# A chunked attention with a channel mix: the opening's mixes taken from TensorE to VectorE, and another order of its steps

## The chip, the cores and the metric

The kernel runs on one core of a Trainium2 chip. The metric is the device time of one execution in microseconds (us). The core's engines are TensorE (PE; its weight loads are PEld), VectorE (DVE), ScalarE (ACT), GpSimd (POOL) and SyncE (SP), which here issues nearly all DMAs. Each engine has a queue of its own and works through it in order; between engines there are semaphores.

## The reference, cut to what matters

```python
# q, k, v: (8, 8, 576, 64); attention inside chunks of 64 tokens
scores = (q_c @ k_c.T) / 8;  attn = softmax(scores)      # + 1e-9 in the denominator
x = (attn @ v_c), heads side by side                     # (8, 576, 512)
x_prev = x moved by one token, zero at the first of a batch row
xk = mu_k * x + (1 - mu_k) * x_prev
xr = mu_r * x + (1 - mu_r) * x_prev
out = sigmoid(xr @ w_r) * (relu(xk @ w_k) ** 2 @ w_v)    # w_k 512x1024, w_v 1024x512, w_r 512x512
```

The three weights come as 64-bit numbers; the kernel reads them as pairs of 32-bit words and builds fp32 values from them.

## The kernel before, in words

The 4608 tokens are worked in 18 groups of 256; a group is two tiles of 128 tokens. The large products run in three passes each, high part by high part, high by low and low by high, so each operand (weights, `xk`, `xr`, the squared values `kk`) is split: a copy rounds the high part (`f_hi`, steps `h...0` of a weight, `.1` of a mix) and a subtraction leaves the low part (`f_lo`).

The program has two stages. The **opening** loads and splits the weights and works tiles 0 to 5 up to their mixes, and groups 0 and 1 to the end. The table `START` (lines 27 to 51) sets its order by hand: each word is a step of a task with the engine that does it (`:A` ACT, `:D` DVE), and the order of the words is the order in which instructions are queued on every engine, the DMA issues on SP among them. After it come groups 2 to 17 in a fixed pattern (`GROUP`), which the diff leaves alone. The opening's tasks are:

- `nq`, `nk`, `v`: loads of q, k and v. `sw...`: load of a weight piece (1024 KB); `cw...`: two passes on ACT (lines 296 and 300) and a shift on DVE (line 303) that turn its words into fp32; `hw...`: its high part (line 141 or 143) and low part (line 314).
- `T`: transposes of q and k on PE (line 358) and the copies out of PSUM. `S`: scores (line 401), row maximum, subtraction, exponential, sum, reciprocal, scaling. `P`: transposed probabilities (465), their copy, the product with v (`xps`, 485), the column of the token before (502, 506) and the copy to `x`.
- `Mk` and `Mr`: the two mixes of a tile. `Mk.0` makes the difference `d = x - x_prev` on DVE (line 553); `Mk.1` and `Mr.0` make the mixes; then high and low parts (`.2`, `.3` of `Mk`, `.1`, `.2` of `Mr`).
- `R`: `pr`, product of `xr` with w_r (line 683) and sigmoid. `K`: `pk`, product of `xk` with w_k (line 629), relu, square, high and low part. `V`: `pv`, product with w_v (line 714).
- `W:n`: n products of a tile of zeros (`warm`, line 1220), whose result nobody reads.

For tiles 0, 1 and 2 (`ON_PE`, line 523) a mix is made on TensorE: `make_diag` writes four sets of diagonal matrices on ACT (step `dg.0`, line 536), and eight products of 128 columns add x by `mu` and `x_prev` by `1 - mu` in PSUM (`mxk` and `mxr`, line 571). For the tiles from 3 on, DVE makes `d` and then a mix by four instructions of 128 columns (line 583; two times as many where a batch row begins inside the tile).

Of the kernel before, what the change touches and what calls it, by code (L numbers as in the profile page):

```python
# [7 lines left out]
F32 = mybir.dt.float32  # L8
# [3 lines left out]
AF = mybir.ActivationFunctionType  # L12
ALU = mybir.AluOpType
# [3 lines left out]
P = 128  # L17
CH = 64
TT = 128
# [5 lines left out]


START = """
W:9 mu.0:A nq0.0 nk0.0 T0.0 T0.2 T0.1:A swr1.0 P0.3:D T0.3:A nk1.0 nq1.0 T0.4 T0.5:A swr0.0
T0.6 T0.7:A W:4 S0.0 S0.1:D S0.2:D S1.0 W:4 T1.4 S1.1:D v0.0 T1.6 S1.2:D cwr1.1:A S0.3:A S0.4:D
S0.5:D cwr1.0:A T1.5:A W:3 T1.0 S1.3:A S1.4:D S1.5:D P0.0 T1.7:A cwr1.2:D T1.2 cwr0.0:D P1.0  # L30
T1.1:A mu.1 P0.1:A T1.3:A cwr0.1:A nq2.0 P0.2 P1.1:A S2.0 T2.2 S3.0 P0.4:D P1.3:D S2.1:D v1.0
S2.2:D mu.2:A dg.0:A S3.1:D T2.0 swk0.0 S2.3:A cwr0.2:D Mk0.1 S3.2:D T2.3:A P1.2 S2.4:D
hwr1.0:A Mk1.0:D Mk0.0:D nk2.0 Mk0.2:A cwk0.0:A swk2.0 S2.5:D Mr0.0 swk1.0 cwk0.1:A P1.4:A
T2.1:A S3.3:A T2.6 Mr0.1:A hwr1.1:D Mk0.3:D P2.3:D hwr0.0:A P2.0 cwk0.2:D Mr0.2:D Mk1.1 swk3.0
Mk1.2:A Mk1.3:D T2.7:A hwr0.1:D T2.4 Mr1.0 hwk0.0:D P2.1:A Mr1.1:D hwk0.1:D R00.0 cwk2.0:A
Mr1.2:D v2.0 S3.4:D cwk1.1:A T2.5:A Mk2.0:D cwk1.0:A swv2.0 S3.5:D v3.0 cwk1.2:D cwk3.1:A P2.2
R01.0 P2.4:A cwk2.1:A K00.0 swv0.0 R00.1:A P3.3:D R01.1:A cwk3.0:A cwk2.2:D P3.0 P3.1:A K00.1:A
hwk2.0:A Mr2.0 P3.2 hwk1.0:A cwk3.2:D Mr2.1:A S4.0 P3.4:A Mk2.1 hwk2.1:D S5.0 hwk1.1:D cwv2.0:A
cwv2.1:A hwk3.0:A swv1.0 K01.0 K01.1:A K01.2:A Mk3.0:D Mr3.0:D K02.0 K00.2:A cwv2.2:D hwk3.1:D
v4.0 Mk3.1:D Mr2.2:D S4.1:D Mr3.1:A K03.0 cwv1.1:A Mr3.2:D cwv1.0:A bk3.0 Mk2.2:D Mk2.3:D  # L40
K00.3:A R10.0 S5.1:D Mk3.2:A cwv0.1:A K01.3:A hwv2.0:A K00.4:D K02.1:A K02.2:A K01.4:D K02.3:A
P4.3:D cwv0.0:A R10.1:A Mk3.3:D hwv2.1:D R11.0 K03.1:A K02.4:D K03.2:A R11.1:A K10.0 K10.1:A
swv3.0 K10.2:A cwv0.2:D K11.0 cwv1.2:D hwv0.0:A K03.3:A S4.2:D K13.0 hwv1.0:A hwv0.1:D cwv3.1:A
bq3.0 S5.2:D cwv3.0:A K10.3:A K03.4:D v5.0 hwv1.1:D V001.0 cwv3.2:D S4.3:A K13.1:A V001.1
V001.2 hwv3.0:A K10.4:D V001.3 V001.4 S4.4:D K13.2:A S4.5:D V001.5 P4.0 hwv3.1:D S5.3:A V001.6
V001.7 P4.1:A S5.4:D K13.3:A S5.5:D P4.2 K11.1:A K13.4:D D7.1:D v7.0 P5.0 P4.4:A K11.2:A
V001.8:D K12.0 V10.0 V001.9:D V11.0 K11.3:A V11.1 P5.1:A Mk4.0:D Mk4.1:D K12.1:A P5.2 K12.2:A
P5.3:D K12.3:A K11.4:D V10.1 D6.1:D K12.4:D P5.4:A Mr4.0:D V10.2 V10.3 V11.2 V11.3 Mk5.0:D
V10.4 Mk5.1:D Mr4.1:A V11.4 D7.0:D Mk4.2:A V10.5 v6.0 V10.6 V11.5 V10.7 Mk5.2:A Mk4.3:D Mr4.2:D
Mk5.3:D Mr5.0:D Mr5.1:A V11.6 D6.0:D V11.7 V11.8:D Mr5.2:D V10.8:D  # L50
"""


# [26 lines left out]
def tile_chunk_attention_channel_mix(  # L80
# [12 lines left out]
    nc = tc.nc  # L93
    B_, H, S, D = q.shape
# [3 lines left out]
    NB = DM // P  # L98
# [16 lines left out]
    mx = pool("mx")  # L115
# [4 lines left out]
    mo = pool("mo", 2)  # L120
# [3 lines left out]
    ps_o = ctx.enter_context(tc.tile_pool(name="ps_o", bufs=2, space=PSUM))  # L124

    do = Steps()
    T = {}
# [5 lines left out]
    ident = const.tile([P, P], F32, name="ident")  # L133
    make_identity(nc, ident)
    mus = mo.tile([2 * NB, P], F32, tag="relu", name="mus")
    mu2 = par.tile([P, 2, 2, NB], F32, name="mu2")
# [10 lines left out]
    def queue(e):  # L147
        return nc.scalar if e == "A" else nc.sync
# [81 lines left out]
    def load_mu():  # L230
        do.task = "mu"

        def fn(e):
            for i, mu in enumerate((mu_k, mu_r)):
                queue(e).dma_start(
                    out=mus[i * NB : (i + 1) * NB], in_=mu.rearrange("(c p) -> c p", p=P)
                )

        def f_tr(_):
            T["mu"] = ps_k.tile([P, 2 * NB], F32, tag="k", name="mu_t")  # L240
            nc.tensor.transpose(out=T["mu"], in_=mus, identity=ident[: 2 * NB, : 2 * NB])

        def f_move(e):

            x = T["mu"].rearrange("p (i c) -> p i c", i=2)
            nc.scalar.activation(mu2[:, 0], x, AF.Copy)
            nc.scalar.activation(mu2[:, 1], x, AF.Copy, scale=-1.0, bias=1.0)

        do(fn, "A")
        do(f_tr, "P")  # L250
        do(f_move, "A")
# [197 lines left out]
    def x_cuts(t):  # L449

        cut = -t * TT % S
        if 0 < cut < TT:
            return [(0, cut, 0), (cut, TT - cut, cut + 1)]
        return [(0, TT, 0)]
# [65 lines left out]

    ON_PE = (0, 1, 2)
    diag = {}

    def make_diag():
        do.task = "dg"

        def fn(e):
            for i, nm in enumerate("kr"):  # L530
                for n in range(2):
                    to = diag[nm, n] = mo.tile([P, NB, P], F32, tag="mix", name=f"diag_{nm}{n}", bufs=4)
                    for cb in range(NB):
                        col = mu2[:, n, i, cb : cb + 1]
                        if e == "A":
                            nc.scalar.activation(to[:, cb], ident, AF.Copy, scale=col)
                        else:
                            nc.vector.tensor_scalar(to[:, cb], ident, col, None, ALU.mult)

        do(fn, "D")  # L540

    def x_mix(t):
        g, tl = divmod(t, 2)
        do.task = f"Mk{t}"
        part = slice(tl * TT, (tl + 1) * TT)

        def f_d(e):
            if t in ON_PE:
                return
            d = T[f"d{t}"] = mo.tile([P, NB, TT], F32, tag="mix", name=f"d_{t}", bufs=4)  # L550
            x = xt[t]
            for s, m, c in x_cuts(t):
                engine[e].tensor_tensor(
                    d[:, :, s : s + m],
                    x[:, :, c + 1 : c + 1 + m],
                    x[:, :, c : c + m],
                    ALU.subtract,
                )

        do(f_d, "D")  # L560
        for nm, mu in (("k", muk), ("r", mur)):

            def f_mix(e, nm=nm, mu=mu):
                x = xt[t]
                if t in ON_PE:
                    m = T[f"m{nm}{t}"] = ps_o.tile([P, NB, TT], F32, tag="o", name=f"mx{nm}_{t}")
                    for cb in range(NB):
                        for s, w, c in x_cuts(t):
                            for n in range(2):
                                c0 = c + 1 - n  # L570
                                nc.tensor.matmul(  # L571
                                    m[:, cb, s : s + w],
                                    diag[nm, n][:, cb],
                                    x[:, cb, c0 : c0 + w],
                                    start=(n == 0),
                                    stop=(n == 1),
                                )
                    return
                m = T[f"m{nm}{t}"] = mo.tile([P, NB, TT], F32, tag="mix", name=f"mix{nm}_{t}", bufs=4)
                d = T[f"d{t}"]  # L580
                for cb in range(NB):
                    for s, w, c in x_cuts(t):
                        nc.vector.scalar_tensor_tensor(
                            out=m[:, cb, s : s + w],
                            in0=d[:, cb, s : s + w],
                            scalar=mu[:, cb : cb + 1],
                            in1=x[:, cb, c : c + w],
                            op0=ALU.mult,
                            op1=ALU.add,
                        )  # L590

            def f_hi(e, nm=nm):
                if f"x{nm}{g}" not in T:
                    T[f"x{nm}{g}"] = [
                        (kp if nm == "k" else rp).tile([P, NB, G], F32R, tag=f"{nm}{s}", name=f"x{nm}{s}_{g}")
                        for s in ("hi", "lo")
                    ]
                copy(e, T[f"x{nm}{g}"][0][:, :, part], T[f"m{nm}{t}"])

            def f_lo(e, nm=nm):  # L600
                hi, lo = T[f"x{nm}{g}"]
                engine[e].tensor_tensor(
                    lo[:, :, part], T[f"m{nm}{t}"], hi[:, :, part].bitcast(F32), ALU.subtract
                )

            do.task = f"M{nm}{t}"
            do(f_mix, "D")
            do(f_hi, "A")
            do(f_lo, "D")
# [563 lines left out]


    load_mu()
    make_diag()
    for t in range(6):
        if t % 2 == 0:
            load_nat(t // 2)
# [35 lines left out]
    with tc.manual_schedule():  # L1215
        for word in START.split():
            name, _, e = word.partition(":")
# [3 lines left out]
            else:  # L1221
                fn, engine_of = first.pop(name)
# [100 lines left out]
```

## Time and profile before

| | us |
|---|---|
| median of 3 runs (lowest to highest) | 572.79 (572.33 to 573.97) |
| the profiled execution, its own time | 574.04 |
| span of that execution in the trace | 572.0 |
| busy: PE, DVE, ACT, POOL | 564.0, 452.8, 356.3, 0.7 |
| first `pr` product starts at | 39.47 |
| the opening's last product ends, and group 2's pattern begins, at | 104.22 |

All times below are from the span's start. A busy time is the sum of the engine's own instructions. In the timeline a number in brackets is the idle time of the engine before the row and what ended it; a row's first number is the start, the second how long the row's instructions took from the first start to the last end, and since instructions overlap at their edges, the step from one row's start to the next is what a row costs its engine.

### The profile page before, as it was taken

To read this page: it belongs to the slowest core of one execution; us is meant where nothing else is said; L and a number is where in the kernel's file an instruction comes from. 1 tells how busy PE (TensorE), PEld (TensorE's weight loads), DVE (VectorE), ACT (ScalarE), POOL (GpSimd) and SP (SyncE) were. 2 spreads that over 40 slices of the span, in tenths; PEclk is the share of its full clock that TensorE was granted. 3 is DMA by queue.
4 is the path that set the end of the run, shared out by engine and by line. 5 is a ranking of instruction groups with operands and counts; after the bars stand their busy time and mean duration, and the time that the engine had idled before them with its cause. 6 is when DMAs were issued, how large, how long until landed. Compare 5 with 4: busy or idle time off the path is not lost.

```text
span 572.0 us, 15372 instructions
## 1 busy us (share of the span) xinstructions
PE 564.0 (99%) x6499; PEld 536.0 (94%) x6499; DVE 452.8 (79%) x753; ACT 356.3 (62%) x535; POOL 0.7 (0%) x6
## 2 busy tenths in 40 slices
PE   8899999999999999999999999999999999999997
PEld 7789999999999999999999999999999999999997
DVE  1597878899988888878787878887888788977834
ACT  4798975472938393929292929293838384747462
POOL 0000000000000000000000000000000000000000
PEclk9899999999999999999999999999999999999999
DMA  9998152343444343330234343434343411011011
GB/s 287 220 315 200 52 110 75 85 70 69 105 90 87 93 64 95 64 94 1 77 56 101 65 96 53 99 58 97 64 84 67 74 44 40 37 39 38 1 38 38
DMA packets 184276, 49.25 MB, mean 86 GB/s; under 512 B 169608, under 2 KB 176272, under 8 KB 184208
## 3 DMA queue, kind: packets, MB, share of 16 engines
q1 hardware_dynamic: 183904, 48.01, 37.3%
q8 instruction: 51, 0.84, 0.6%
q10 hardware_dynamic: 304, 0.27, 0.1%
q14 instruction: 17, 0.14, 0.1%
HBM read 38.80 MB, written 9.44 MB: 84 GB/s over the span
## 4 chain that ended last, share of the span: by engine, by line
PE 97%; DVE 2%; ACT 0%; issue 0%
PE pk L629 35%; PE pr L683 17%; PE vx L903 15%; PE vyz L903 11%; PE pv L714 6%; PE xps L1091 3%; PE s L1006 3%; PE pt L1073 2%; PE warm L1220 1%; PE trq L358 1%; PE trk L358 1%; PE s L401 1%; PE mxk L571 1%; PE mxr L571 1%; PE pt L465 0%; PE xps L485 0%
## 5 line engine op out<-in xcount | busy, mean ns | idle before, releaser
L629 PE MATMUL pk<-xkhi,wk 128*128 128x256 f32 (+1 forms) x1166 | 201.8, 276 | 0.0
L629 PEld LDWEIGHTS pk<-xkhi,wk 128*128 128x128 f32 x1166 | 176.8, 188 | 0.3
L629 PE MATMUL pk<-xklo,wk 128*128 128x256 f32 x576 | 160.0, 278 | 0.0
L629 PEld LDWEIGHTS pk<-xklo,wk 128*128 128x128 f32 x576 | 108.3, 188 | 0.1
L650 ACT ACTIVATE rr<-pk 128x512 f32<-128x512 f32 x60 | 35.3, 588 | 114.4 <-PE pk L629 114.4
L683 PE MATMUL pr<-wr,xrhi 128*128 128x512 f32 x288 | 90.4, 395 | 0.0
L903 PE MATMUL vx<-b,ks 128*128 128x256 f32 x540 | 68.5, 276 | 0.0
L903 PE MATMUL vyz<-b,kk 128*128 128x256 f32 x540 | 68.5, 276 | 0.0
L903 PEld LDWEIGHTS vyz<-b,kk 128*128 128x128 f32 x540 | 64.5, 188 | 0.0
L903 PEld LDWEIGHTS vx<-b,ks 128*128 128x128 f32 x540 | 64.5, 188 | 0.0
L683 PEld LDWEIGHTS pr<-wr,xrhi 128*128 128x128 f32 x288 | 52.7, 188 | 10.2
L683 PE MATMUL pr<-wr,xrlo 128*128 128x512 f32 x144 | 56.2, 390 | 0.0
L932 ACT ACTIVATE u<-vx 128x256 f32<-128x256 f32 x30 | 11.5, 384 | 54.3 <-PE vx L903 54.3
L741 DVE TENSOR_TENSOR kk<-rr,kk 128x1024 fp32r<-128x1024 f32 x30 | 35.4, 1222 | 10.7 <-ACT kk L887 10.6
L657 ACT ACTIVATE rr<-rr 128x512 f32<-128x512 f32 x60 | 38.0, 633 | 1.9
L741 DVE TENSOR_TENSOR xklo<-mk,xkhi 128x1024 fp32r<-128x1024 f32 x15 | 18.4, 1225 | 24.7 <-ACT xkhi L1163 24.7
L714 PE MATMUL pv<-b,kk 128*128 128x256 f32 x288 | 33.9, 277 | 0.0
L714 PEld LDWEIGHTS pv<-b,kk 128*128 128x128 f32 x288 | 33.1, 188 | 0.1
L683 PEld LDWEIGHTS pr<-wr,xrlo 128*128 128x128 f32 x144 | 27.0, 188 | 5.7
L741 DVE TENSOR_TENSOR ks<-ss,ks 128x512 fp32r<-128x512 f32 x45 | 28.3, 683 | 0.0
L1153 DVE SCALAR_TENSOR_TENSOR mk<-d,mu,x 128x256 f32<-128x256 f32 (+3 forms) x80 | 27.7, 414 | 0.4
L1153 DVE SCALAR_TENSOR_TENSOR mr<-d,mu,x 128x256 f32<-128x256 f32 (+3 forms) x80 | 27.5, 410 | 0.0
(127 smaller groups left out, 857.3 us busy)
## 6 DMA issues: line engine op xcount, KB each, us to landing
v<-in_v SPq DMA_DIRECT2D x144, 64.0 KB, 2.5
out<-sg SPq DMA_DIRECT2D x34, 256.0 KB, 2.5
q_ring<-in_q SPq DMA_DIRECT2D x192, 36.0 KB, 2.0
k_ring<-in_k SPq DMA_DIRECT2D x192, 36.0 KB, 2.1
wk_st<-in_moe_w_k SPq DMA_DIRECT2D x4, 1024.0 KB, 11.9
wv_st<-in_moe_w_v SPq DMA_DIRECT2D x4, 1024.0 KB, 7.5
wr_st<-in_moe_w_r SPq DMA_DIRECT2D x2, 1024.0 KB, 9.9
q_ring<-in_q SPq DMA_DIRECT2D x2, 512.0 KB, 6.7
```

What stands on the lines that cost most here:

```text
L358: nc.tensor.matmul(x[halves[j], hp, :], T[f"{nm}{g}"][:, j * HP + hp, r, :], ident, start=True, stop=True,)
L629: nc.tensor.matmul(pk[:, e, part], wk[a][:, cb, f * P : (f + 1) * P], xk[b][:, cb, part], start=(n == 0 and part is parts[0]), stop=(n == ...
L650: nc.scalar.activation(r, T[f"pk{g}{fp}"], AF.Relu)
L657: nc.scalar.activation(r, r, AF.Square)
L683: nc.tensor.matmul(pr, xr[a][:, cb, tl * TT : (tl + 1) * TT], wr[b][:, cb, :], start=(n == 0), stop=(n == 3 * NB - 1),)
L714: nc.tensor.matmul(T[f"pv{g}{tl}"][:, cols[c]], kk[a][:, f, tok[tl]], quarter(f // HF, c)[:, b, f % HF, :], start=(f == 0 and n == 0 and c ...
L741: nc.vector.tensor_tensor(to, x, y, ALU.subtract)
L903: nc.tensor.matmul(to, a[i][:, f, :], weight(w, j, f), start=first and f == 0 and n == 0, stop=f == HF - 1 and n == 2, skip_group_check=True,)
L932: nc.scalar.activation(T[f"u{g}"][n // 2][:, n % 2], src(), AF.Copy)
L1006: nc.tensor.matmul(T[f"s{g}"][halves[e], j, tl, hp, :], qT[halves[j], hp, cols], kT[halves[j], hp, cols], start=True, stop=True,)
L1091: nc.tensor.matmul(T[f"xps{g}"][halves[c], 2 * j + a, tl * TT + e * CH : tl * TT + (e + 1) * CH], T[f"v{2 * g + tl}"][halves[j], hp, e, :] ...
L1153: nc.vector.scalar_tensor_tensor(out=to[:, cb, s : s + w], in0=T[f"d{g}"][:, cb, s : s + w], scalar=mu[:, cb : cb + 1], in1=T[f"xg{g}"][:, ...
```

## The change

`ON_PE`, `make_diag` and the PE branch of `f_mix` go, so that tiles 0, 1 and 2 are mixed on DVE as the others are; so does the instruction that made `1 - mu`. `START` is written anew, all of it. Of 296 words of the table before, `dg.0` is gone; 23 others name another engine or now need one. The idle products are 33 instead of 20, at other places. The low parts of the weights stand on DVE before and after.

```diff
 START = """
-W:9 mu.0:A nq0.0 nk0.0 T0.0 T0.2 T0.1:A swr1.0 P0.3:D T0.3:A nk1.0 nq1.0 T0.4 T0.5:A swr0.0
...
+mu.0:A nk0.0 nq0.0 swr0.0 W:9 T0.4 T0.6 T0.5:A swr1.0 T0.7:A T0.2 T0.3:D nk1.0 T0.0 mu.1 T0.1:A
...
             nc.scalar.activation(mu2[:, 0], x, AF.Copy)
-            nc.scalar.activation(mu2[:, 1], x, AF.Copy, scale=-1.0, bias=1.0)
...
-    ON_PE = (0, 1, 2)
...
-    def make_diag():
...
         def f_d(e):
-            if t in ON_PE:
-                return
...
             def f_mix(e, nm=nm, mu=mu):
                 x = xt[t]
-                if t in ON_PE:
...
-                                nc.tensor.matmul(
-                                    m[:, cb, s : s + w],
-                                    diag[nm, n][:, cb],
-                                    x[:, cb, c0 : c0 + w],
...
-    make_diag()
```

Steps that change between ACT and DVE once DVE's row maximum of tile 0 has begun: from ACT to DVE `Mr2.1`, `K01.2`, `K03.3`, `hwv3.0` (two instructions), `K13.3`, `K11.1`, `K12.1`, `K12.2`, `Mk4.2`, `Mk5.2`, `Mr5.1`; from DVE to ACT `P0.4`, `hwk0.0`, `Mr1.1`, `Mk2.2`.

PE, from the product with v of tile 0 on, before (the first number in a name is the group, or for `trq0`, `trq1` the row of a pair and then the group; `mxk_0` is the mix of tile 0):

```order
L485 MATMUL xps_0_314<-pT_0_308,v_0_242 64x64 x16
L401 MATMUL s_1_332<-kT_123,qT_122 64x64 x16
L358 MATMUL trq1_2_349<-ident_109,q_ring_116 64x128 x8
L401 MATMUL s_1_332<-kT_123,qT_122 64x64 x16
L358 MATMUL trq0_2_408<-ident_109,q_ring_116 64x128 x8
L571 MATMUL mxk_0_421<-x_0_160,diag_k0_387 128x128
L571 MATMUL mxk_0_421<-x_0_160,diag_k1_392 128x128
```

and PE from the same product on in the change:

```order
L484 MATMUL xps_0_292<-pT_0_287,v_0_214 64x64 x16
L357 MATMUL trq0_1_320<-ident_109,q_ring_116 64x128 x8
L357 MATMUL trq1_1_329<-ident_109,q_ring_116 64x128 x8
L464 MATMUL pt_0_275<-ident_109,p_0_210 128x128 x4
L1183 MATMUL warm_108<-idle_106 128x128 x3
L400 MATMUL s_1_372<-kT_123,qT_122 64x64 x16
L1183 MATMUL warm_108<-idle_106 128x128 x5
L400 MATMUL s_1_372<-kT_123,qT_122 64x64 x16
L484 MATMUL xps_0_292<-pT_0_287,v_1_344 64x64 x16
L647 MATMUL pr_0_0_440<-wr0_120,xrhi_0_363 128x512
```

The mixes are gone from PE, the transposes of group 2's q and k stand behind the first `pr` instead of ahead of it, and the first `pr` follows the product with v of tile 1 directly.

DVE around the low part of w_r's first piece, before:

```order
L435 TENSOR_TENSOR p_1_383<-p_1_383,z_2_448 128x512
L314 TENSOR_TENSOR wr1_121<-wr1_st_158,wr0_120 128x1024
L602 TENSOR_TENSOR xklo_0_456<-mxk_0_421,xkhi_0_455 128x4x128
L506 COPY x_1_491<-x_0_160 128x4
L303 SCALAR_TENSOR_TENSOR wk0_st_417<-wk0_st_417 128x1024
L602 TENSOR_TENSOR xrlo_0_487<-mxr_0_462,xrhi_0_486 128x4x128
```

and in the change (`d_0`, `mixr_0`, `mixk_0` belong to tile 0, `z_1` and `p_0` to the probabilities of tile 1):

```order
L313 TENSOR_TENSOR wr1_121<-wr0_st_130,wr0_120 128x1024
L428 TENSOR_REDUCE z_1_311<-p_0_210 128x8
L429 TENSOR_SCALAR z_1_311<-z_1_311 128x8
L430 RECIPROCAL z_1_311<-z_1_311 128x8
L531 TENSOR_TENSOR d_0_317<-x_0_206 128x512
L434 TENSOR_TENSOR p_0_210<-p_0_210,z_1_311 128x512
L547 SCALAR_TENSOR_TENSOR mixr_0_339<-d_0_317,mu2_115,x_0_206 128x128 x4
L547 SCALAR_TENSOR_TENSOR mixk_0_355<-d_0_317,mu2_115,x_0_206 128x128 x4
```

The difference and both mixes of tile 0 now stand in DVE's queue, between the softmax of tile 1 and the low parts.

SP's first loads before (w_r, q, k and v; `x4` is the four parts of a v tile):

```order
L184 DMA q_ring_116<-in_q 128x8x128
L184 DMA k_ring_117<-in_k 128x8x128
L292 DMA wr1_st_158<-in_moe_w_r 128x2x1024
L184 DMA k_ring_117<-in_k 128x8x128
L184 DMA q_ring_116<-in_q 128x8x128
L292 DMA wr0_st_175<-in_moe_w_r 128x2x1024
L199 DMA v_0_242<-in_v 64x4x64 x4
```

and in the change:

```order
L184 DMA k_ring_117<-in_k 128x8x128
L184 DMA q_ring_116<-in_q 128x8x128
L291 DMA wr0_st_130<-in_moe_w_r 128x2x1024
L291 DMA wr1_st_160<-in_moe_w_r 128x2x1024
L184 DMA k_ring_117<-in_k 128x8x128
L199 DMA v_0_214<-in_v 64x4x64 x4
L184 DMA q_ring_116<-in_q 128x8x128
L291 DMA wk3_st_281<-in_moe_w_k 128x4x512
L199 DMA v_1_344<-in_v 64x4x64 x4
L291 DMA wk0_st_349<-in_moe_w_k 128x4x512
```

Both pieces of w_r come ahead of the second k, and two pieces of w_k ahead of the q and k of group 2.

## Rows read from the trace of the kernel before

**Rows 1.** The page: busy time and share, then the chain by engine

```profile
PE 564.0 (99%) x6499; PEld 536.0 (94%) x6499; DVE 452.8 (79%) x753; ACT 356.3 (62%) x535; POOL 0.7 (0%) x6
...
PE 97%; DVE 2%; ACT 0%; issue 0%
```

**Rows 2.** Windows: stretch, length, busy PE, PEld, DVE, ACT, POOL, clock, DMA, GB/s

```profile
11.43:39.47 28.04, 24.49 (x379) 21.44 (x380) 19.18 (x32) 23.16 (x45) 0.00 (x0) 0.94 1.03 280
39.47:70.00 30.53, 30.53 (x325) 27.86 (x323) 23.54 (x40) 27.46 (x37) 0.00 (x0) 1.00 0.57 131
70.00:104.22 34.22, 34.22 (x350) 33.70 (x348) 26.67 (x61) 21.36 (x36) 0.00 (x0) 1.00 0.39 93
104.22:140.00 35.78, 35.78 (x452) 34.21 (x452) 33.50 (x43) 17.44 (x25) 0.00 (x0) 1.00 0.45 81
```

**Rows 3.** Timeline of PE: start, us, line, op, out<-in, records, idle before

```profile
12.90 0.69 PE L401 MATMUL s<-kT,qT 64*64 64x64 f32 x32 [1.54 <-DVE p L421]
13.52 1.16 PE L1220 MATMUL warm<-idle 128*128 128x128 f32 x8
14.61 1.97 PE L358 MATMUL trk<-ident,k_ring 128*64 128x128 f32 x32
...
21.35 0.69 PE L485 MATMUL xps<-pT,v 64*64 64x64 f32 x32 [0.53 <-ACT pT L141]
23.35 1.04 PE L401 MATMUL s<-kT,qT 64*64 64x64 f32 x32 [1.31 <-ACT pT L141]
24.32 1.97 PE L358 MATMUL trq<-ident,q_ring 128*64 128x128 f32 x16
26.23 0.99 PE L401 MATMUL s<-kT,qT 64*64 64x64 f32 x32
27.15 1.09 PE L358 MATMUL trq<-ident,q_ring 128*64 128x128 f32 x16
28.18 2.05 PE L571 MATMUL mxk<-x,diag_k 128*128 128x128 f32 x16
30.16 0.69 PE L485 MATMUL xps<-pT,v 64*64 64x64 f32 x32
...
39.47 0.70 PE L683 MATMUL pr<-wr,xrhi 128*128 128x512 f32 x2
...
52.11 2.05 PE L571 MATMUL mxk<-x,diag_k 128*128 128x128 f32 x16
54.09 0.69 PE L401 MATMUL s<-kT,qT 64*64 64x64 f32 x32
```

**Rows 4.** Windows around the stretch in which the granted clock was low

```profile
23.35:27.00 3.65, 3.65 (x78) 3.20 (x80) 0.00 (x0) 3.63 (x15) 0.00 (x0) 0.53 1.10 292
27.00:30.00 3.00, 3.00 (x48) 2.76 (x40) 2.67 (x4) 2.50 (x8) 0.00 (x0) 1.00 1.07 325
```

**Rows 5.** Timeline of DVE: a row maximum, a mix, and two instructions that follow

```profile
11.43 0.69 DVE L413 TENSOR_REDUCE m<-s 128x8 f32<-128x512 f32 x1 [10.41 <-PE s L401]
...
54.56 1.14 DVE L583 SCALAR_TENSOR_TENSOR mixr<-d,mu,x 128x128 f32<-128x128 f32 x4
55.62 1.22 DVE L303 SCALAR_TENSOR_TENSOR wv_st<-wv_st 128x1024 int32<-128x1024 int32 x1
...
63.93 0.69 DVE L602 TENSOR_TENSOR xklo<-mxk,xkhi 128x512 fp32r<-128x512 f32 x1
64.54 0.68 DVE L413 TENSOR_REDUCE m<-s 128x8 f32<-128x512 f32 x1
```

**Rows 6.** Timeline of ACT: half of the diagonal matrices

```profile
25.82 2.43 ACT L536 ACTIVATE diag_r<-ident,mu 128x128 f32<-128x128 f32 x8
```

**Rows 7.** Windows of the first 30 us, read for their last number, GB/s

```profile
0.00:20.00 20.00, 17.37 (x236) 15.57 (x236) 7.50 (x15) 9.93 (x13) 0.70 (x6) 1.00 0.93 257
20.00:30.00 10.00, 8.16 (x151) 7.07 (x149) 3.53 (x6) 8.78 (x25) 0.00 (x0) 0.83 0.97 265
```

More of the change, by code (lines that the diff above doesn't have):

```diff
@@ L27 @@
 START = """
-W:9 mu.0:A nq0.0 nk0.0 T0.0 T0.2 T0.1:A swr1.0 P0.3:D T0.3:A nk1.0 nq1.0 T0.4 T0.5:A swr0.0
[L29 to L50, printed above, removed]
+mu.0:A nk0.0 nq0.0 swr0.0 W:9 T0.4 T0.6 T0.5:A swr1.0 T0.7:A T0.2 T0.3:D nk1.0 T0.0 mu.1 T0.1:A
@@ new lines @@
+cwr0.1:A W:1 S0.0 cwr0.0:A P0.3:D S0.1:D S0.2:D S0.3:A cwr0.2:D v0.0 S0.4:D W:7 S1.0 nq1.0 W:5
+T1.6 S1.1:D cwr1.1:A mu.2:A S0.5:D S1.2:D T1.4 P0.0 hwr0.0:A swk3.0 cwr1.0:A T1.7:A S1.3:A
+cwr1.2:D P0.1:A W:3 P0.2 T1.5:A hwr0.1:D S1.4:D P0.4:A hwr1.0:A Mk0.0:D S1.5:D T1.0 T1.2 T1.1:A
+Mr0.0:D v1.0 swk0.0 P1.0 Mk0.1:D T1.3:A P1.3:D P1.1:A Mr0.1:A nk2.0 cwk3.0:A W:3 S2.0 Mr0.2:D
+S2.1:D nq2.0 W:5 S3.0 P1.2 P1.4:A hwr1.1:D v2.0 S2.2:D R00.0 S2.3:A cwk0.0:A T2.4 cwk3.1:A
+S3.1:D Mk1.0:D S2.4:D Mr1.0:D cwk0.1:A S2.5:D T2.5:A T2.6 S3.2:D swk2.0 swk1.0 Mk0.2:A Mr1.1:A
@@ new lines @@
+P2.0 T2.7:A T2.2 Mk1.1:D cwk0.2:D T2.0 Mk0.3:D P2.1:A Mk1.2:A S3.3:A Mr1.2:D T2.3:A P2.2
+cwk3.2:D hwk0.0:A hwk0.1:D Mk1.3:D T2.1:A S3.4:D P2.3:D hwk3.0:A cwk2.0:A cwk2.1:A S3.5:D
+hwk3.1:D P2.4:A v3.0 R01.0 cwk2.2:D cwk1.1:A P3.3:D cwk1.0:A K00.0 K00.1:A P3.0 cwk1.2:D
+hwk2.0:A K03.0 P3.1:A S4.0 hwk1.0:A Mk2.0:D hwk2.1:D P3.2 K03.1:A swv1.0 K00.2:A P3.4:A v5.0
+Mr2.0:D K03.2:A hwk1.1:D Mr2.1:D S5.0 Mk2.1:D K02.0 R00.1:A Mk3.0:D Mr2.2:D cwv1.0:A swv0.0
+Mr3.0:D swv2.0 K00.3:A Mk3.1:D K01.0 K00.4:D R01.1:A cwv1.1:A Mk2.2:A K03.3:D Mr3.1:A Mr3.2:D
@@ new lines @@
+v4.0 K01.1:A Mk3.2:A K03.4:D K01.2:D Mk2.3:D Mk3.3:D cwv2.0:A cwv2.1:A K02.1:A R10.0 cwv2.2:D
+cwv0.0:A R11.0 K10.0 S4.1:D cwv1.2:D K02.2:A K11.0 cwv0.1:A hwv2.0:A K01.3:A cwv0.2:D K01.4:D
+hwv0.0:A P4.3:D bq3.0 K10.1:A K10.2:A hwv2.1:D K12.0 hwv1.0:A swv3.0 R10.1:A hwv0.1:D S4.2:D
+R11.1:A S5.1:D V001.0 S4.3:A hwv1.1:D S5.2:D V001.1 V001.2 V001.3 S4.4:D K02.3:A K10.3:A S4.5:D
+S5.3:A K02.4:D cwv3.0:A S5.4:D P4.0 V001.4 cwv3.1:A S5.5:D K12.1:D P4.1:A cwv3.2:D P5.0
+hwv3.0:D P5.1:A V001.5 P4.2 hwv3.1:D K12.2:D P5.2 K12.3:A P4.4:A K10.4:D bk3.0 K11.1:D Mk4.0:D
@@ L51 @@
+V001.6 K11.2:A V001.7 K11.3:A K13.0 D7.0:D V001.9:D K11.4:D P5.3:D V001.8:D K12.4:D V11.0 V11.1
+V10.0 v6.0 Mr4.0:D K13.1:A V10.1 K13.2:A V10.2 P5.4:A K13.3:D V10.3 V11.2 V10.4 Mk4.1:D Mk5.0:D
+K13.4:D V10.5 V11.3 V11.4 V11.5 Mk4.2:D V11.6 Mk5.1:D Mr4.1:A Mr4.2:D V10.6 v7.0 D7.1:D V11.7
+D6.0:D Mk4.3:D D6.1:D Mk5.2:D Mr5.0:D V11.8:D Mk5.3:D Mr5.1:D V10.7 V10.8:D Mr5.2:D
 """
@@ L519, in att_values @@
         do(f_x, "A")
-    ON_PE = (0, 1, 2)
-    diag = {}
-    def make_diag():
[L527 to L540, printed above, removed]
     def x_mix(t):
@@ L564, in f_mix @@
                 x = xt[t]
-                if t in ON_PE:
[L566 to L570, printed above, removed]
-                                nc.tensor.matmul(
-                                    m[:, cb, s : s + w],
-                                    diag[nm, n][:, cb],
-                                    x[:, cb, c0 : c0 + w],
[L575 to L578, printed above, removed]
                 m = T[f"m{nm}{t}"] = mo.tile([P, NB, TT], F32, tag="mix", name=f"mix{nm}_{t}", bufs=4)
```

## The prediction, made before the changed kernel was run

> **What bounds the kernel now.** I read the page first: PE is busy for 564.0 of 572.0 us, and 97% of the chain that ended last is PE [rows 1]. So the span is PE's work plus PE's waits, and a change counts by what it does to either. The windows by stage come next [rows 2]: from the first `pr` at 39.47 on PE is busy for the whole of every stretch (30.53 of 30.53, 34.22 of 34.22, 35.78 of 35.78), so its waits all lie ahead of 39.47, and what the change can win lies in the opening, which ends at 104.22. Last I read PE's own timeline there [rows 3]. It shows three things to be won: the mixes on PE, three waits in brackets, and a stretch in which rows of one kind take longer than the same kind elsewhere. DVE is the engine to watch. It was idle for 28.04 - 19.18 = 8.86, 6.99 and 7.55 us of the opening's three stretches, and for only 2.28 of the 35.78 us behind it [rows 2].
>
> **Mixes removed from PE.** The first `mxk` costs 1.98 us from its start at 28.18 to the next row at 30.16, the last one 1.98 (52.11 to 54.09) [rows 3]. There are six such groups (two mixes of three tiles), the other four cost between 1.81 and 1.98, and all six 11.6 us. PE has no cover for them, so their whole cost leaves PE's work: **-11.6**.
>
> **The low clock.** [...] PE had waited 0.53 and 1.31 us just before [rows 3]. In it, one group of transposes took 1.91 us (24.32 to 26.23) where the next took 1.03 (27.15 to 28.18), and two halves of scores took 0.97 and 0.92 where the half at 12.90 took 0.62 [rows 3]: 0.88 + 0.35 + 0.30 = 1.5 us. In the change the waits there are filled with eleven idle products and with the two groups of transposes that now follow tile 0's product with v, so I take the stretch as gone: **-1.5**, with 0 as the other end.
>
> **Old waits and new idle products.** The three waits of 1.54, 0.53 and 1.31 us [rows 3] make 3.4 us, and the places where they stood now hold other work: -3.4. There are 33 idle products instead of 20; four of them cost 13.52 to 14.61 = 1.09 us [rows 3], so 13 more cost 13 x 0.27 = **+3.5**. The two cancel: the idle products are waits under another name. Work that is only moved past the first `pr` (the transposes of group 2, the transposed probabilities of tile 2) costs PE the same on either side.
>
> PE's own sum is thus -11.6 - 1.5 - 3.4 + 3.5 = -13.0 us, plus whatever PE has to wait anew for the engines that feed it.
>
> **What DVE takes over.** Per tile one difference and two mixes. A 512-wide instruction of two tensors costs 64.54 - 63.93 = 0.61 us, a mix 55.62 - 54.56 = 1.06 [rows 5]; 0.61 + 2 x 1.06 = 2.73, and three tiles 8.2. Of steps that change between ACT and DVE behind 11.43, twelve 512-wide instructions come to DVE and four leave it: eight times 0.61 = 4.9. DVE's work in the opening grows by 13.1 us. Its idle time from 11.43 to 104.22 was 8.86 + 6.99 + 7.55 = 23.4 us [rows 2], and it can't begin earlier, since its first row maximum needs the first scores, whose loads and transposes stand where they stood. So if DVE never idled any more and all its opening work ended with the opening, the opening could be 23.4 - 13.1 = 10.3 us shorter and no more. PE would gain 13.0 without that limit, so new waits of **at least 2.7** are to be expected. ACT is no such limit: it loses both rows of diagonal matrices, 2.43 us for one [rows 6], and eight steps on balance, and was idle for 4.88 + 3.07 + 12.86 = 20.8 us of the opening [rows 2].
>
> **How much PE waits.** That is the one term with no row of its own. The lower bound is the 2.7 above; it could be undercut only by DVE work that slides past the opening, at most the 2.28 us that DVE idles from 104.22 to 140 [rows 2], which gives 0.4. For the upper bound I take DVE's best-filled stretch in the trace, the same one: 2.28 of 35.78 is 6.4% idle [rows 2]. An opening that ends ten microseconds earlier has DVE at work for some 82 us, 6.4% of them is 5.2, and 2.7 + 5.2 = 7.9. I take **+3.6**, near the lower bound, for a reason in the order: what DVE does last in the opening are mixes and low parts of tile 5, which PE wants only in the stretch behind, so the opening need not end with DVE. At the front, where the change puts DVE's wait on x of tile 0, the difference of tile 0 stands behind the shift and the low part of w_r, so that wait has cover; if w_r were late, the cover would be gone and that wait would cost what x is late.
>
> **Loads.** DVE and ACT now wait for weights earlier, so I check what lands when. The DMA engines moved 257 GB/s in the first 20 us and 265 in the next ten [rows 7]: 5.14 MB by 20 and 7.79 by 30. In the new order w_r, both k and q of groups 0 and 1, both v and two pieces of w_k make 6.5 x 1.05 = 6.8 MB, down by 26.3 us. The first `pk` stands behind two `pr` and the transposes, at 35 or later, and its weights take one shift and one low part on DVE (1.2 us each) and three passes on ACT. Some 3 us are left. Moving the loads past each other on SP thus costs nothing unless they are slower by more than that.
>
> **The sum.** -13.0 + 3.6 = -9.4 us. Made against the profiled execution it is 572.0 - 9.4 = 562.6 for the span, 564.6 for its own time of 574.04. That execution was 1.25 us over the median, so against the median of 572.79 I forecast **563.4**.
>
> **Rivals.**
> *DVE sets the pace.* DVE's idle share stays what its best stretch shows, PE waits 7.9, the gain is 13.0 - 7.9 = 5.1: **567.7**. For it: DVE's queue is in order, and its first steps on each weight wait for a landing and for ACT, with every mix behind them. Against it: the new order gives DVE softmax work of tiles 1 to 3 to do in between, and in the trace the 20 us in which DVE idled most (11.43 to 39.47) are just those which the mixes now fill.
> [...]
> *A late load holds DVE's queue, and the kernel gets slower.* The shift of the first w_k piece stands on DVE ahead of the low parts of both tiles of group 0, so if that piece lands late, both `pr` and all `pk` wait behind it. It decides from the point where PE's new waits pass 13.0 us, that is when the piece lands some 3 + 13 = 16 us after 26.3; at 18 us late it costs 15 and the result is **574.8**. Against it: 7.79 MB were down by 30 us [rows 7], and the order of the loads alone doesn't take bandwidth away.
> *The change doesn't shorten the opening.* If PE's gap were only refilled, because scores, softmax and landings set the first `pr` near 36, the gain would be the 3 us between: **569.8**. Against it: ahead of the first `pr` at 39.47 PE was busy for 24.49 of 28.04 us [rows 2], largely with work that is now gone or behind it.
>
> **How the numbers follow.** The forecast has a chance of 0.70, DVE's pace 0.16, the clock 0.08, the late load 0.03, the refilled gap 0.03. The range reaches to DVE's pace above (567.7) and to the lower bound of the waits below (13.0 - 0.4 = 12.6 gained, 560.2, of which I leave out the last part): 560.9 to 568.0. It holds the forecast's own spread, the clock's case and DVE's pace at its price; what lies beyond these prices, with the last two rivals, I put at 2 in 10. A measurement of this kernel can tell about 0.3%, 1.7 us, from no change. Faster by more than that: the first three, 0.94, and the part of the refilled gap's case that lies over 1.7 us, 0.95 in all; slower 0.03, and 0.02 within.
>
> **What would show it.** Right: the first `pr` starts at 25 to 28 (39.47 less four mixes, 7.7, four groups of transposes now behind it, 4 x 1.03, and the low clock's 1.5, is 26.2), no L571 rows, the opening's last product ends near 95, DVE is idle for under 3 us between 11 and 95, PE's waits behind the first `pr` sum to 1 to 4 us and end with DVE or ACT. Groups 2 to 17 take as long as before. Wrong: a first `pr` past 31, waits of PE on DVE that go on into the stretch behind the opening, or a granted clock under 1 in more than one stretch of the opening.

## The result, and the profile after

The changed kernel takes **562.68 us** (median of 6 runs, 562.42 to 562.91); the kernel before, run beside it, 572.85 (572.33 to 574.07). The ratio is **0.9818**, 95% interval 0.9805 to 0.9831: 1.8% faster. The forecast was 563.4 with a range from 560.9 to 568.0. The profiled execution after took 562.54 us with a span of 560.8, and lies at its kernel's median; the one before lay 1.25 over its own. So the spans differ by 11.2 us, the medians by 10.2.

The page after: busy time by engine, and the chain by engine, to be held against [rows 1].

```profile
PE 554.0 (99%) x6429; PEld 526.6 (94%) x6429; DVE 462.8 (83%) x789; ACT 346.0 (62%) x509; POOL 0.7 (0%) x6
...
PE 90%; ACT 7%; DMA 2%; DVE 0%; issue 0%; ACTq 0%
```

Windows of both kernels, the opening from DVE's first row maximum on and the rest (stretch, length, busy PE, PEld, DVE, ACT, POOL, clock, DMA, GB/s). Before:

```profile
11.43:104.22 92.79, 89.24 (x1048) 83.00 (x1048) 69.39 (x131) 71.97 (x116) 0.00 (x0) 0.98 0.64 162
104.22:572.00 467.78, 464.53 (x5331) 443.52 (x5330) 383.18 (x620) 279.50 (x413) 0.00 (x0) 1.00 0.32 67
```

and after:

```profile
10.85:92.93 82.08, 79.89 (x983) 74.35 (x983) 78.42 (x165) 62.53 (x92) 0.00 (x0) 1.00 0.76 184
92.93:560.80 467.87, 464.55 (x5331) 443.53 (x5330) 383.51 (x622) 279.44 (x413) 0.00 (x0) 1.00 0.32 66
```

The rest takes 467.8 us in both, so all of the gain lies in the opening, which ends 11.3 us earlier. These rows split it: 0.6 because the first row maximum begins earlier (only half of it is shown to come from the change, as told further down), 9.35 of PE's busy time (89.24 to 79.89), and 1.4 of PE's idle time (3.55 to 2.19). DVE took on 9.0 us of work in a stretch 10.7 us shorter: its idle time fell from 23.4 to 3.7 us.

PE's timeline after, around the first `pr` and at the opening's end (start, us, line, op, out<-in, records, idle before):

```profile
22.15 0.69 PE L400 MATMUL s<-kT,qT 64*64 64x64 f32 x32
22.77 1.38 PE L1183 MATMUL warm<-idle 128*128 128x128 f32 x10
24.18 0.69 PE L400 MATMUL s<-kT,qT 64*64 64x64 f32 x32
24.69 0.65 PE L484 MATMUL xps<-pT,v 64*64 64x64 f32 x32
25.27 0.73 PE L647 MATMUL pr<-wr,xrhi 128*128 128x512 f32 x2
...
92.93 1.16 PE L970 MATMUL s<-kT,qT 64*64 64x64 f32 x64
```

No mix stands there any more; the halves of scores take 0.69 us each, where two of them took 1.04 and 0.99 in [rows 3]; the first `pr` begins at 25.27 instead of 39.47. What PE still waits for, all of its waits up to 140 us (us in total, times, longest; the first one is the start of the program):

```profile
PE warm L1183 <- DVE idle L130: 1.1, 1, 1.1
PE trk L357 <- DMA k_ring<-in_k: 1.0, 1, 1.0
PE pt L464 <- DVE p L434: 0.5, 1, 0.5
PE s L400 <- ACT pT L141: 0.3, 1, 0.3
PE pk L593 <- ACT relu L614: 0.2, 1, 0.2
PE s L400 <- ACT qT L141: 0.2, 1, 0.2
```

### The profile page after: what moved, and what is told of

It is laid out like the page before. It is cut to its first block, busy times and chain, and to the rows that moved or that the text cites. A ratio compares the mean times of both kernels' runs of the same rounds, so it can differ in the third digit from the quotient of the medians.

```text
span 560.8 us, 15239 instructions
## 1 busy us (share of the span) xinstructions
PE 554.0 (99%) x6429; PEld 526.6 (94%) x6429; DVE 462.8 (83%) x789; ACT 346.0 (62%) x509; POOL 0.7 (0%) x6
## 4 chain that ended last, share of the span: by engine, by line
PE 90%; ACT 7%; DMA 2%; DVE 0%; issue 0%; ACTq 0%
PE pk L593 32%; PE pr L647 16%; PE vx L867 15%; PE vyz L867 11%; PE pv L678 6%; PE xps L1055 3%; PE s L970 3%; PE pt L1037 2%; DMA k_ring<-in_k 2%; PE warm L1183 1%; ACT wk L141 1%; ACT wv_st L295 1%; PE trk L357 1%; ACT wv_st L299 1%; ACT relu L614 0%; ACT wk_st L299 0%
## 5 line engine op out<-in xcount | busy, mean ns | idle before, releaser
L647 PEld LDWEIGHTS pr<-wr,xrhi 128*128 128x128 f32 x288 | 52.7, 188 | 10.3
L705 DVE TENSOR_TENSOR kk<-rr,kk 128x1024 fp32r<-128x1024 f32 x30 | 35.4, 1222 | 10.7 <-ACT kk L851 10.6
```

What stands on the lines that cost most here:

```text
L647: nc.tensor.matmul(pr, xr[a][:, cb, tl * TT : (tl + 1) * TT], wr[b][:, cb, :], start=(n == 0), stop=(n == 3 * NB - 1),)
L705: nc.vector.tensor_tensor(to, x, y, ALU.subtract)
```

## The experiments

The theory: the gain is PE's work (mixes and slow stretch gone), the order's part is to give DVE the mixes early enough that PE doesn't wait for them; what limits now is DVE. Rivals: the order alone makes the gain, by better overlap; or the idle products matter; or a load does. Ratios are against the kernel before, run on the same chip.

**The mixes alone.** The order of before, with the mixes on DVE:

```diff
-S2.2:D mu.2:A dg.0:A S3.1:D
+S2.2:D mu.2:A S3.1:D
...
-Mk0.1 S3.2:D
+Mk0.0:D Mk0.1 S3.2:D
```

and likewise `Mk1.0` moved ahead of `Mk1.1`, `Mk2.0` ahead of `Mr2.0`, and `Mr2.2` ahead of `Mk3.1`.

> The mixes of tiles 0 to 2 go to VectorE as in the change, but the order of the opening stays that of before (four words moved, so that a difference comes ahead of its mixes and a buffer is free in time). Theory (TensorE's work falls by 11.6 us, but only an order that gives VectorE the mixes early turns that into time): VectorE gets 8.2 us more in a queue laid out without them, ahead of the w_k parts; TensorE, which never waits behind the first pr in the kernel before, waits there for 6 to 10 us in all; 569 to 577 us, so no gain worth the name. Rival (taking work off the engine that bounds is enough): 561 to 564 us, waits behind the first pr under 3 us.

Measured: 578.7 us, ratio 1.0093 (1.0074 to 1.0112), above the theory's range. The same mixes taken off PE make the kernel 0.9% *slower*. The two largest waits of PE:

```profile
PE pr L647 <- DVE wr L313: 4.7, 1, 4.7
PE pt L464 <- DVE p L434: 3.7, 1, 3.7
```

DVE's timeline ahead of the longest one, which ended at 43.64:

```profile
39.21 0.68 DVE L531 TENSOR_TENSOR d<-x 128x512 f32<-128x512 f32 x1
39.92 1.14 DVE L547 SCALAR_TENSOR_TENSOR mixk<-d,mu,x 128x128 f32<-128x128 f32 x4
41.76 0.69 DVE L566 TENSOR_TENSOR xklo<-mixk,xkhi 128x512 fp32r<-128x512 f32 x1 [0.70 <-ACT xkhi L141]
42.37 1.22 DVE L313 TENSOR_TENSOR wr<-wr_st,wr 128x1024 fp32r<-128x1024 f32 x1
```

The low part of w_r stands in DVE's queue behind the difference and a mix of tile 1, and behind a wait for ACT. Meanwhile the granted clock fell:

```profile
33.90:47.60 13.70, 7.81 (x30) 5.71 (x31) 12.93 (x27) 10.47 (x15) 0.00 (x0) 0.50 1.07 315
```

At a granted clock of 1.00 PE would have saved up to about half of the 7.81 us that it worked there, 3.9 (an estimate: one group of transposes in [rows 3] took 1.91 us where the granted clock was 0.53 and the next 1.03 where it was 1.00, [rows 4]). On the pages PE's idle time grew from 572.0 - 564.0 = 8.0 to 576.8 - 556.8 = 20.0 us, and its busy time fell by 7.2 us and not by the 11.6 of the mixes. The difference of 4.4 is put down to the low clock, near its estimate: -11.6 + 4.4 + 12.0 = +4.8, by which the span grew. Behind the first `pr` PE waited for 7.2 us, within the theory's 6 to 10; the low clock was not in the theory. So taking work from PE gains nothing by itself; it needs the rewritten order. Which part of that order counts (the places in the queues, the steps that go to another engine, or the loads) no run separates.

**PE's time given back.** After, with eleven idle products behind each of four places where the old kernel had a mix on PE:

```diff
-Mr0.0:D v1.0
+Mr0.0:D W:11 v1.0
```

and the same behind `Mk0.1:D`, `Mr1.0:D` and `Mk1.1:D`.

> The changed kernel with TensorE's load given back: four times eleven idle products (44 x 0.27 = 11.9 us) where the mixes of tiles 0 and 1 are queued, two of the four ahead of the first pr and two behind it. Theory (TensorE's work is what the time is made of): they fill the 2 us or so of waits that the changed kernel has and cost the rest, 6 to 10 us: 569 to 573 us. Rival (the gain comes from the new order, which starts the weights and the first pr earlier, and not from the mixes): under 565 us.

Measured: 570.35 us, ratio 0.9946 (0.9929 to 0.9964), so 7.3 us of the gain are gone. One of the four places in PE's timeline (an idle product makes two records, so 22 records are eleven products):

```profile
33.58 2.72 PE L1183 MATMUL warm<-idle 128*128 128x128 f32 x22
36.23 1.09 PE L357 MATMUL trk<-ident,k_ring 128*64 128x128 f32 x16
```

Eleven products cost 36.23 - 33.58 = 2.65 us. On the pages PE is busy for 564.1 us instead of 554.0, so all 44 cost some 10.1; the waits behind the first scores vanish in exchange (none is left but 0.2), and the span grows by 568.7 - 560.8 = 7.9. So the order alone is not the gain: with PE's time put back, most of it goes.

**No idle products.** After, with `W:9` alone left of the `W` words.

> The changed kernel without its idle products, but for the nine at the start. Theory (they stand in waits for softmax and copies): each becomes a wait of the same length, the first pr starts where it did (25.3 us), and the time is 562 to 563.5 us. [...]

Measured: 563.14 us, ratio 0.9820 (0.9803 to 0.9838), the same as after. The granted clock did fall, twice:

```profile
14.30:17.70 3.40, 3.40 (x29) 2.79 (x24) 3.40 (x5) 2.34 (x4) 0.00 (x0) 0.50 1.10 339
24.50:27.90 3.40, 3.26 (x67) 2.95 (x68) 3.08 (x5) 1.21 (x3) 0.00 (x0) 0.50 1.09 197
```

and waits stood where the idle products had been, the three largest being

```profile
PE s L400 <- DVE p L420: 1.5, 1, 1.5
PE trk L357 <- DMA k_ring<-in_k: 1.5, 2, 1.1
PE s L400 <- DVE m L412: 1.3, 1, 1.3
```

The time is the theory's, though the granted clock, which is 1.00 all through the opening of after, falls to 0.50 without the idle products. The first `pr` began at 26.55 and the opening ended at 93.83, 0.9 later than after; against that the span grew by 0.8 and the ratio by 0.0002. The pages tell why so little is left. The 24 products that are gone cost 6.75 us in after, but PE's busy time fell by only 554.0 - 550.4 = 3.6, so the other 3.1 are put down to the low clock (an estimate: at 0.50, half of the 6.66 us that PE worked in the two stretches, 3.3). PE's idle time grew by 4.4 us, from 6.8 to 11.2. The waits are thus shorter than the products in whose place they stand, against the theory, and the low clock takes back what that saves.

**The load that PE waits for, earlier.** `nk2.0` (k of group 2) moved ahead of `swk0.0` (a piece of w_k):

```diff
...
-swk0.0 P1.0 Mk0.1:D T1.3:A P1.3:D P1.1:A Mr0.1:A nk2.0
+nk2.0 swk0.0 P1.0 Mk0.1:D T1.3:A P1.3:D P1.1:A Mr0.1:A
...
```

> The changed kernel with the k of group 2 loaded ahead of the w_k piece that precedes it, so that the one wait of TensorE for a load (1.0 us, at 29.3) goes. Theory (the DMA engines run full until 52 us, so a load that is moved up moves another back): the wait turns up again at the first products with w_k, and the time is 562.5 to 564.5 us. Rival (the place of that one load costs 1.0 us): 561.5 to 562 us.

Measured: 565.17 us, ratio 0.9860 (0.9839 to 0.9882), 2.4 us *slower* than after. PE's wait for k is gone, and two others stand in its place. First PE's timeline, then ACT's, which tells why:

```profile
33.29 1.09 PE L357 MATMUL trq<-ident,q_ring 128*64 128x128 f32 x16 [1.67 <-ACT kT L141]
34.83 1.09 PE L357 MATMUL trq<-ident,q_ring 128*64 128x128 f32 x16 [0.44 <-ACT kT L141]
```

```profile
29.51 1.19 ACT L295 ACTIVATE wk_st<-wk_st 128x1024 f32<-128x1024 f32 x1 [2.44 <-DMA wk_st<-in_moe_w_k]
30.60 2.13 ACT L299 ACTIVATE wk_st<-wk_st 128x1024 int32<-128x1024 uint32 x2
32.63 0.60 ACT L141 ACTIVATE kT<-trk 128x512 f32<-128x512 f32 x1
```

ACT waits for the weight piece, which is now later, and the copy `kT` that PE needs stands behind its three passes. The rival (the wait for k was worth its 1 us) fell. The theory had the direction; the size was too small (564.5 at most) and the place another, since the wait stands ahead of q's transposes and not at the products with w_k. On the pages PE's idle time grew by 1.2 us and its busy time by 1.2. The idle time is what the edit explains; 0.7 of the busy time lie ahead of the first row maximum, before the load that was moved, and what the rest is no run shows.

**More and less work on DVE.** First the differences of tiles 0 to 2 made three times, 3.7 us of DVE work more:

```diff
-                engine[e].tensor_tensor(
+                for _ in range(3 if t < 3 else 1):
+                    engine[e].tensor_tensor(
...
```

> The changed kernel with the difference of tiles 0, 1 and 2 made three times instead of once: six more VectorE instructions of 0.61 us, 3.7 us of work for nothing. Theory (VectorE is filled to the brim in the opening, so what it gets more TensorE waits for): 2 to 4 us longer, 564.7 to 567 us. Rival (the 3.7 us for which VectorE is still idle between 11.4 and 94 take it up): 562.5 to 563.3 us.

Measured: 566.93 us, ratio 0.9886 (0.9865 to 0.9908), 3.9 us over after. PE's two long waits, and behind the first one two halves of scores:

```profile
22.11 0.66 PE L464 MATMUL pt<-ident,p 128*128 128x128 f32 x4 [1.94 <-DVE p L434]
...
23.91 1.13 PE L400 MATMUL s<-kT,qT 64*64 64x64 f32 x32
...
26.82 0.69 PE L400 MATMUL s<-kT,qT 64*64 64x64 f32 x32
...
34.32 0.63 PE L464 MATMUL pt<-ident,p 128*128 128x128 f32 x4 [1.49 <-DVE p L420]
```

A window of it, in which after has a granted clock of 1.00:

```profile
11.40:26.00 14.60, 12.56 (x204) 11.24 (x204) 14.09 (x29) 11.34 (x17) 0.00 (x0) 0.89 1.15 285
```

The span grew by 564.5 - 560.8 = 3.7 us. On the pages 2.1 of them are idle time of PE (8.9 instead of 6.8), and 1.6 are busy time for the same number of products, put down to the clock, which fell behind the first wait (0.89 in this window, in which one half of scores took 1.13 us and the other 0.69). That the cost equals the work put in is thus chance: 3.7 us of work made 2.1 us of waits, and behind one of these the clock fell.

Then the mixes of tiles 0 to 2 left out, 6.4 us less:

```diff
+                if t < 3:
+                    T[f"m{nm}{t}"] = T[f"d{t}"]
+                    return
...
```

> The changed kernel with the mixes of tiles 0, 1 and 2 left out (the difference is passed on as the mix, so the output isn't the reference's): 6.4 us less on VectorE, nothing else changed. Theory (the waits that TensorE has left end with a load, with copies on ScalarE and with the softmax, and the order is cut to them): 562 to 562.7 us. Rival (VectorE sets the pace of the changed kernel): 559 to 561 us, as the 2 us of waits go.

Measured: 562.52 us, ratio 0.9807 (0.979 to 0.9825): the same as after. A window from 40 us on:

```profile
40.00:60.00 20.00, 19.81 (x231) 18.58 (x230) 17.30 (x28) 19.98 (x29) 0.00 (x0) 1.00 0.70 176
```

PE is busy for 19.81 of 20 us, and ACT for 19.98. With less work on DVE there is little for PE to win: some 2 us of waits are left after. The half microsecond before `pt` stays. The 1.0 us for k is not there in this execution, in which the transposes of that k begin at 28.75, 0.5 earlier than after; but its first scores came 0.5 later than after, so the span differs by only 0.5. So the sharper form of the theory, "DVE bounds the opening", holds on one side only: DVE is full enough that added work shows at once, and PE is full enough that removed work hardly does.

## Why the prediction was right, and where its steps were off

**Mixes off PE, low clock, idle products.** -11.6, -1.5 and +3.5 make -9.6; on the page PE's busy time fell by 564.0 - 554.0 = 10.0. The idle products behind the first nine cost, by the steps of the timelines, 6.75 us after (24 of them) against 3.03 before (eleven), so +3.7. The giving back of PE's time showed what such work counts for: 10.1 us of it, less 2.2 us of idle time that it filled, made the span 7.9 us longer.

**The low clock.** In the profiled execution after, no stretch is below 1.00, where before the one of [rows 4] was at 0.53; the 1.5 us are gone. A fall of the clock, to which the prediction gave 0.08, didn't come about here, but it did in three of the experiments: the mixes alone (0.50 from 33.90 to 47.60, with PE's wait of 4.7 us in it), no idle products (0.50 in two stretches, the longest wait 1.5 us), and more work on DVE (0.89 from 11.40 to 26.00, with a wait of 1.94 us in it). The profiled execution after, with waits of 1.1 us and less, never shows it. A wait of 1.67 us in the kernel with k earlier left the clock at 1.00 in its profile, so the length of one wait alone doesn't decide it here; what does, no run shows.

**The term that was mis-sized: how much PE waits.** The prediction took 3.6 us with a lower bound of 2.7. PE's idle time from the first scores on is 2.2, under the bound. That bound came from a ledger of DVE: 23.4 us idle, less 13.1 us of new work, so an opening at most 10.3 us shorter. From the first row maximum it is 92.79 - 82.08 = 10.7 shorter, and DVE still idles for 3.7. The step that was off is the 13.1: it measured 78.42 - 69.39 = 9.0. One cause is in the groups of DVE by kind (xcount | busy, mean ns | idle before). Before, the high parts that were cast on DVE came out of PSUM, or were weights of 1024 columns:

```profile
L143 DVE CAST xkhi<-mxk 128x512 fp32r<-128x512 f32 x1 | 0.7, 692 | 2.4 <-PE pk L629 2.4
L143 DVE CAST wk<-wk_st 128x1024 fp32r<-128x1024 f32 x1 | 0.7, 684 | 0.0
```

After, seven casts of 512 columns read SBUF, these four, two of `b` and one of `xrhi`:

```profile
L143 DVE CAST kk<-relu 128x512 fp32r<-128x512 f32 x2 | 0.8, 425 | 0.0
L143 DVE CAST xkhi<-mixk 128x512 fp32r<-128x512 f32 x2 | 0.8, 402 | 0.0
```

They last 0.40 to 0.43 us. What one costs its engine shows in DVE's timeline of the kernel with the mixes alone:

```profile
45.16 0.42 DVE L143 CAST xrhi<-mixr 128x512 fp32r<-128x512 f32 x1
45.49 1.22 DVE L313 TENSOR_TENSOR wk<-wk_st,wk 128x1024 fp32r<-128x1024 f32 x1
```

The step is 0.33, not the 0.61 of an instruction of two tensors, so seven of them cost about 2.0 us less than the prediction took; the row of `wk`, with twice the columns in the time of one, could have told. At 512 columns a cast took 692 ns out of PSUM before and 402 to 425 out of SBUF after; why they differ, no run shows. The other cause is that busy time doesn't add. Summed over DVE's groups (each counts the overlaps inside itself once), the opening's work grew from about 73.8 to 85.6 us, by 11.8; the engine's busy time, in which all overlapping ends count once, by 9.0. The overlaps between groups thus grew from 4.4 to 7.2 us: in the fuller queue more time is shared by an instruction and the one ahead of it. An example are these rows, after,

```profile
14.23 0.20 DVE L430 RECIPROCAL z<-z 128x8 f32<-128x8 f32 x1
14.35 0.64 DVE L412 TENSOR_REDUCE m<-s 128x8 f32<-128x512 f32 x1
```

and before, where the scaling follows its own reciprocal:

```profile
15.91 0.20 DVE L431 RECIPROCAL z<-z 128x8 f32<-128x8 f32 x1
16.15 0.69 DVE L435 TENSOR_TENSOR p<-p,z 128x512 f32<-128x512 f32 x1
```

The reciprocal costs 0.12 us with an unrelated instruction behind it and 0.24 with one that needs it. That this is why the overlaps grew is argued from such rows; no run tested it. A third part is small: some 0.3 us of DVE's work slid behind the opening's end (383.18 to 383.51 in the rest), for which the prediction had allowed 0.4.

**The end of the waits.** Behind the first `pr` they sum to 1.6 us (1 to 4 foretold). They were to end with DVE or ACT; the longest, 1.0 us, ended with a DMA, the k of group 2. It isn't there in every profile (the kernel with less work on DVE has none).

**The rest.** The first `pr` came at 25.27 (25 to 28 foretold), groups 2 to 17 take as long as before, the opening's last product ends near 93 (95 foretold). DVE idles for 3.7 us of the opening (under 3 foretold). The first row maximum begins 0.6 us earlier, which the prediction denied ("it can't begin earlier"). Half of that is the change: the prediction had looked at the loads and transposes and missed what stands between these and the first scores. Before:

```profile
7.68 1.97 PE L358 MATMUL trk<-ident,k_ring 128*64 128x128 f32 x32
9.58 1.16 PE L1220 MATMUL warm<-idle 128*128 128x128 f32 x8
10.66 0.69 PE L401 MATMUL s<-kT,qT 64*64 64x64 f32 x32
```

and after:

```profile
7.39 1.97 PE L357 MATMUL trq<-ident,q_ring 128*64 128x128 f32 x32
9.29 0.22 PE L241 MATMUL mu_t<-ident,mus 8*128 8x8 f32 x1
9.44 0.49 PE L1183 MATMUL warm<-idle 128*128 128x128 f32 x2
10.08 0.69 PE L400 MATMUL s<-kT,qT 64*64 64x64 f32 x32 [0.15 <-ACT qT L141]
```

From the start of the second transposes to the first scores it takes 2.69 us instead of 2.98: one idle product stands there instead of four, 0.64 us with the wait behind it instead of 1.08, and `mu_t` adds 0.15. The other 0.3 is that the second transposes begin earlier, and that is not shown to come from the change. In the four other executions that begin with the same instructions (idle products added, k earlier, more and less on DVE) they begin anywhere from 7.23 to 7.94, and the first row maximum comes at 10.70 to 11.39.

A slip in reading: the stretch from 11.43 to 39.47, in which DVE idled most, is 28.04 us long, not "20 us"; no sum uses it.

**What was luck.** The profiled gain is 11.2 us instead of 9.4, and yet the forecast of 563.4 came within 0.7 of the measured 562.68. Two errors offset each other. The low clock's 1.5 us went off as a term, and most of them went off a second time as the 1.25 us by which the profiled execution lay over its median. The runs of the kernel before, made beside the experiments, point to it: the four with a mean granted clock of 1.0 took 572.13 to 572.64 us, the ten with 0.997, the clock of the profiled one, 573.83 to 574.49. So an execution with the slow stretch takes some 1.5 us longer than one without, and the median of 572.79 is near those without. Taken off once, the sum gives 564.6, which is still in the range; the waits (1.4 us less than taken) and PE's busy time (0.4 less) made up for it.

**The rivals.** DVE's pace (7.9 us of waits) was not reached, and the kernel with 3.7 us more on DVE added only 2.1 us of waits. The late load didn't happen: ACT's first pass on the w_k piece began at 26.92, when it had landed, against 26.3 foretold. But the 3 us that the prediction left for loads to be late were not free: in the kernel with k earlier that pass began 2.6 us later, at 29.51, and PE waited 2.1 us behind it, for the copies `kT` in ACT's queue. The opening was not just refilled: given PE's time back, it lengthens by 7.6 us (the end at 100.53, against 92.93).

## What to carry to other kernels

When work moves from a full engine to one with idle time, ask where in the second engine's queue it will stand: the same move made this kernel 0.9% slower in the old order and 1.8% faster in the new. Before a term found in one execution is taken off a median, look whether the median's executions have it. Work out what the engine takes over by kind (one tensor or two, SBUF or PSUM: here a step of 0.33 us for a cast of one tensor in SBUF against 0.61 for an instruction of two, and 692 ns for a cast out of PSUM), and don't make a hard bound out of summed busy times: here the overlaps grew from 4.4 to 7.2 us with the fuller queue. DVE, filled to 96% of the opening, was a bound for additions here (3.7 us more work, a span 3.7 us longer) and not for removals (6.4 us less, the same time).

## What the runs showed that was not expected

- Of the 3.7 us by which six more instructions on DVE lengthened the span, only 2.1 are waits of PE; 1.6 are PE's own work, put down to the low clock behind one of these waits (0.89 from 11.40 to 26.00).
- Two stretches of 3.4 us at a granted clock of 0.50, with PE busy in 6.66 of the 6.80 us, left the time the same (0.9820): the 24 idle products left out there had cost 6.75 us, and in their place came 4.4 us of idle time and some 3 us more of busy time. In the old order with the mixes on DVE, one stretch of 13.70 us at 0.50 cost about 4 (an estimate: 11.6 of mixes taken off, 7.2 less busy time).
- A load issued earlier, for a wait of 1.0 us, made the kernel 2.4 us slower; 1.2 of it is more idle time of PE, as new waits came up behind ACT's queue.
- Executions that begin with the same instructions differ by 0.7 us in when the first row maximum begins (10.70 to 11.39), more than the 0.6 us between the profiles before and after.
